# Sixth tile of theta and sixth mixing step of batch 0 on split operands

## The chip, the cores and the metric

The kernel runs on one core of a Trainium2 chip. The metric is the time of one execution on the device in microseconds; the number given is the median of several runs. 0.5% of it is about 2.2 us.

## The reference

Four batches of 768 tokens, 8 heads of 64: local attention (a window of 16 to each side) together with attention to block summaries (maximum of k and mean of v over 32 tokens), then a mixing layer. All inputs are fp32.

```python
scores_l = scale * q @ k.T, kept where |s - t| < 16
scores_s = scale * q @ k_sum.T + log(32)
a = softmax over both;  x = a @ concat(v, v_sum)       # 768 x 512 a batch
theta = x @ w_theta
zr, zi = x * cos(theta), x * sin(theta)
y = w_tok_r @ zr + w_tok_i @ zi                        # over the tokens
u = x + y
out = u + max(u @ w_ch, 0)
```

## The kernel before

**Tiles and stages.** Each batch is 6 tiles of 128 tokens, so there are tiles 0 to 23. A tile goes through scores (L523), softmax on VectorE (L559) and ScalarE (L563), a transpose (L572, copied out at L578), the product with v (L546), normalisation (L586 to L598), a transpose of x (L605, copied out by L309 or L311), theta (L639 or L644), the phase (L655 to L669: rounding to whole turns, then two sines), and z = x times cosine and sine (L674, in two halves of the channels). The mixing of batches 0 and 1 (`mix_step`) takes two halves of the channels, each of six steps, one for every 128 tokens; step s needs z of tile s and the two weight blocks `w_tok_r` and `w_tok_i` of these rows. A step is four operations on TensorE. Batches 2 and 3 are mixed in `mix_fast`, with sums of weights made beforehand (`weight_sums`) and streamed from HBM through `s_scratch` (L817). At the end comes the product with `w_ch` (L922).

**Plain and split operands.** A product can be made in two ways. Plain: fp32 operands, one matmul instruction of the program, which the trace shows as two records. Split: each operand is a rounded part (`hi_op`, a cast, L309 or L311) and the rest (`lo_op`, a subtraction, L318), and three matmuls stand in place of one. The weights come as 64-bit floats and are first made fp32 on chip (`to_f32`: L401, L405, L407, L409, L412). Two numbers in TUNE say where the split starts: tiles from RT on have theta split, steps from RM on have z and weights split. Both are 6, so batch 0's six tiles of theta and the six steps of its first mixing half are plain; its second half is split already. The weights of theta are split ahead of tile RT (`theta`); those of a plain step are split after that step (`split_wt`), in time for the second half.

**Where things lie.** Fp32 weights of two blocks share one of twelve slots `wt`; from there each pair is written to `f_scratch` (768 KB), to be read by `weight_sums`. The temporaries of `to_f32` and the loads of k and v for the next batch's summaries (L444, L465) share three buffers `f`. Theta's fp32 weights lie in the four buffers `xh`, `xl`, which afterwards hold the split x. TensorE's results lie in PSUM; GpSimd does not read them.

**Order.** Every operation has a number, in the order in which the program states it. ORDER lists all numbers in the order of issue, with a letter where the engine is chosen by hand (a, d, g; without one, ScalarE where it can, then VectorE). Each engine works through its operations in that order, waiting for whatever one needs; all transfers are issued by one queue (SP), in that order too. Where VectorE and GpSimd both use SBUF (`port`), a GpSimd operation listed right after a VectorE one waits for it.

Of the kernel before, what the change touches and what calls it, by code (L numbers as in the profile page):

```python
# [17 lines left out]
B, H, S, D = 4, 8, 768, 64  # L18
# [36 lines left out]
17g 8 0g 1g 31 23 27 25 9 24 18 29 10 28 2 26 39 3 19 32 30 20 4 44g 33 5 6g 190g 49g 46 45 48 7 50 86 194g 47 193 51 60 61 34  # L55
35 52 53 79 191 64 239g 192g 87 57 55 62 54 66 13 88 65 185 11 93 14 42 238 63 89 12 36 241g 40 90 59 58 240g 91 100 67 56 80
195 37 38g 235 68 15 92d 188 186 81 69 107 21 82 204 94 71 205 206 108 41g 43d 70 83 209 290 207 95g 187 72 109 84 237 210 196
208 199 76 295g 198 73 197 294g 200 189g 74 77 22 242 203 96 101 75d 102g 201 202 78d 236 251 252 351g 254 212 211 103 213 97
253 104 85 98 215 214 110 223 216 296g 258 224 99d 225 243 255 257 217 118 348g 226 105 227 218 119g 220d 293 256 245 219d 106
244 246 228 247 250 111 120 221 291 121 249 222d 248 123 124g 297 229 122 349g 298 345 259 230 260 262 292 299 261 270 130 125  # L60
301 350g 115 300 271 263 126 272 303 423g 305 302 304 306 273 267d 308 131g 307 116 264d 419 310 135 268 309 265 274 313 127
136g 132 311 312 266d 141 275 269d 314 276 133 315 142g 137 317 316 277 138 352 143 112 231 325 326 318 232 134 327 163 233g
139 144 353 361 168 319d 356 328 320 329 362 278 330 322 355 234 169g 145 331 346 164g 321d 279 364 323 363 282 117 146 324
283 420 332 354 113 347 284 280 365 474 285 147 380 358 114 357 339 165 360 148 366 359 337 166 367 338 149 167 170 368 150
152 381 424 369 422 333 370 400 153 382 128 383 384 171 334 154 172 155 157 281 158g 156 425 385 371 402 401 159 372 386 340
174 335 175g 373 426 392 394 374 421 160 375 377 376 378 387 529 161 404 176 388 379 403 705g 389 454 177 530 179 395 393 178
# [12 lines left out]
795 838g 756 1015 757 690 528g 571 845g 975 765 662 822 759 760 976d 850 691 840 977d 578 846 978 851g 796 768 823 727d 763
184 797 852 946 699 766 758 692 853g 769 1020 701 694d 979 940 702 980 700 941 847g 772 848 693d 579 981 825 767 695 749 696d  # L80
761 762 771 731 753 750 764 580g 798d 824 982 728 770 732 773 983 774 775d 984 947 956 581g 776 854g 777 995 948 729 778d 959
849 781d 949 950 958 725g 582g 802 952 803 996 997 998 953 799g 859 751 943 1016 1021 779 951 782 855 999 730 780 1074 1000
985 860g 1001 856 800 726 963 1018 808 857 1002 942 954 861g 957 961 960 962 801 955 575 826g 783 964 862 863g 1077 858 944g
965 1003 1022 966 1004 986 967d 864g 968 1005 806 804 1017g 810 1031 972 868 805 865g 1050 828 1023 1051d 1052 1032 869g 573
577 987 829 1170 1053 830 1024 866 1025 1033 989g 1006 969d 1054 827 1035 1037 831 1029 1055 870 1028 993 871 1056 1007g 970
872g 1027 1034 867 973 1120d 1038 1008 877 994 1036 1026 1057 1019d 1058 1013 1030 971 1014 974d 873d 1059 1039 874g 1040 1042
1078 878 1041d 809 811 990g 1079 1043 1047d 1208 1076 807 1087 1089 991 876 992 1209 1088 1090 1011 1210d 1083 1094 1093 1044d
1060 879 1009 880 1211 1080 1212 875 881 1082 1129 1012 1045 882g 1048 1213 886 1061 1126 1081 1092 1066 883 1075 1010 884
1084 1091 1214 1063g 1085 887 1067 885 1062 1127 1121 1046d 988 888 1215 1086 1173 1068 1049 1216 895 1095 1096 1098 1106g
1130 1217 1097d 889 1099 1218d 1279 1107g 1280 1281g 1069 1131 1070 896 1071 1228 1133 1100d 1282 1064g 1219 1135 890 1103d  # L90
1229 1283 1072 1073 1139 1065 891g 1137 1132 1110 1141 892 1142 1101 1284 1111 897 1143 1104 1285 1134 1138 1102d 898g 1108
1105d 1145 899g 1146 1286 1140 1144 1136 1109 1287 1128 893 900d 1158d 1147 1148 901g 1150 894 1288 1172 1250 1149d 1118 1174
1289 1114 1175 1112 1151 1305 1116 1178 1179 902 1202 1236 1122 1152 1183 903 1221g 1123 1306 1124 1185 1307 1308g 1187 1177
1181 1309 1153 904 1182 1160 1184 1232 1310 1155 1189 1237 1230 1233 1220g 1188 1176 1125 1186 1311 905 1156 1162 1171 1290
1312 906g 1249 1154 1163 1203 1247 1190 1180 1157 1234 1313 1159g 1191 1192 1193 1291g 1231 1251 1314 1222g 1194d 907 1315d
1252 1254 1195 1235 1292g 1117 1354 1240 1196 1253 1355 1260 1261 1356 1161 1199d 1255 1357g 1166 1168 1319 1197 1358 1198d
1322 1256 1257 1241 1258 1164d 1165g 1169 908g 1316 1263 1242 1200 913 1359 1206 1264 1360 1259 1207 1201d 1243 909 1324 1361
1167 1262 1248 1317g 1267 1382 1599g 1266 1268 1265 1362 1269 910g 1325 1326 1363 1271d 911 1364d 1270 1327 1272 16 1368 1600g
1335 1238 1204 1226 1330 1369d 914g 1328 1463 1370d 1365 915 1387 1276 1371 1366 1205 1367g 912 1273d 1331 1334 1372 1224 1338
916 1595g 1373 1225 1274 1337 1239 1383 1587g 1374 1223 1329 917 1385 1275 1244 918g 919 1245 1293 1596g 1277 1375 1376 1227  # L100
1278 1377 1588g 1333 1388 1320 920 1332 921 1589d 1246g 1339 1294 1297 1321d 1384 1378d 1417 931 1336 1295 1342 1296 1418 1341
1419g 1323 1420 1389 922 1672 1340 1593 1301 1594 1113 1119 1343 923g 1590 1318g 1344 1644 1346 932g 1421 924g 1345 1302 1646
# [71 lines left out]
class Program:  # L174
# [5 lines left out]
    WINDOW, WARM, COOL = 3.41, 0.88, 0.45  # L180
# [99 lines left out]
def attn_moe(tc, qg, kg, vg, kT, vT, vn, wth, wtr, wti, wch, out, tune=TUNE):  # L280
# [4 lines left out]
    K = tune  # L285
# [4 lines left out]
    f_dram = nc.dram_tensor("f_scratch", (NT, P, 2 * S), F32, kind="Internal").ap()  # L290
# [6 lines left out]
    pr = Program()  # L297
# [825 lines left out]
```

## Time and profile before

| | us |
|---|---|
| median of 3 runs | 435.23 (433.77 to 435.77) |
| the profiled execution | 437.3 |
| its span, first to last instruction | 435.6 |
| TensorE busy | 421.7 |
| VectorE busy | 352.2 |
| ScalarE busy | 280.3 |
| GpSimd busy | 209.7 |

The span is 1.7 us shorter than the profiled execution's time. Busy times of TensorE are of pipelined matmuls, with modelled ends, so a full engine is not one at its peak.

### The profile page before, as it was taken

To read this page: it belongs to the slowest core of one execution; us is meant where nothing else is said; L and a number is where in the kernel's file an instruction comes from. 1 tells how busy PE (TensorE), PEld (TensorE's weight loads), DVE (VectorE), ACT (ScalarE), POOL (GpSimd) and SP (SyncE) were. 2 spreads that over 40 slices of the span, in tenths; PEclk is the share of its full clock that TensorE was granted. 3 is DMA by queue.
4 is the path that set the end of the run, shared out by engine and by line. 5 is a ranking of instruction groups with operands and counts; after the bars stand their busy time and mean duration, and the time that the engine had idled before them with its cause. 6 is when DMAs were issued, how large, how long until landed. Compare 5 with 4: busy or idle time off the path is not lost.

```text
span 435.6 us, 10044 instructions
## 1 busy us (share of the span) xinstructions
PE 421.7 (97%) x3682; PEld 350.9 (81%) x3682; DVE 352.2 (81%) x947; ACT 280.3 (64%) x600; POOL 209.7 (48%) x208
## 2 busy tenths in 40 slices
PE   5989999998999999999999999999999989999996
PEld 1455555665888888888888899999899989999996
DVE  3799999778988777875757695866489989999996
ACT  1799995787757784866785885493955447455210
POOL 3543324687775665245465578624453410251542
PEclk9899999999999999999999999999999999999999
DMA  8999956989678678848767987883379696220138
GB/s 294 347 354 364 295 197 208 290 257 322 230 233 273 197 224 266 259 139 247 232 188 223 292 273 218 245 246 119 111 230 338 229 367 223 75 73 20 65 136 289
DMA packets 76321, 100.07 MB, mean 230 GB/s; under 512 B 23024, under 2 KB 58864, under 8 KB 76272
## 3 DMA queue, kind: packets, MB, share of 16 engines
q1 hardware_dynamic: 76272, 99.43, 71.1%
q8 instruction: 29, 0.48, 0.5%
q14 instruction: 20, 0.16, 0.1%
HBM read 75.82 MB, written 23.59 MB: 228 GB/s over the span
## 4 chain that ended last, share of the span: by engine, by line
PE 87%; DMA 10%; DVE 1%; ACT 1%; SPq 0%; issue 0%; POOL 0%; DVEq 0%
PE m L702 25%; PE m L817 19%; PE t L644 11%; PE c L922 7%; PE m L922 6%; PE pa L546 5%; PE s L523 4%; PE t L639 3%; PE t L605 3%; DMA q<-qg 3%; PE pa L572 3%; DMA wth<-wth 2%; DMA wt<-wti 2%; DMA zu<-kT 2%; DMA wt<-s_scratch 1%; PE t L922 1%
## 5 line engine op out<-in xcount | busy, mean ns | idle before, releaser
L817 PE MATMUL m<-wt,hl 128*128 128x384 f32 x504 | 95.7, 339 | 1.4 <-DMA wt<-s_scratch 1.2
L817 PEld LDWEIGHTS m<-wt,hl 128*128 128x128 f32 x504 | 87.7, 188 | 4.9 <-ACT hl L309 1.5
L702 PE MATMUL m<-wt,hl 128*128 128x512 f32 (+1 forms) x432 | 84.9, 341 | 0.0
L702 PEld LDWEIGHTS m<-wt,hl 128*128 128x128 f32 x432 | 68.6, 188 | 10.8
L563 ACT ACTIVATE e<-e,st 128x118 f32<-128x118 f32 x192 | 63.1, 388 | 12.1 <-DVE st L559 11.6
L559 DVE CUSTOM_DVE_ANT_0 e<-s,cs 128x118 f32<-128x118 f32 x192 | 46.8, 272 | 9.6 <-PE s L523 4.7
L318 POOL TENSOR_TENSOR hl<-zu,hl 128x512 fp32r<-128x512 f32 x23 | 30.1, 1309 | 43.9 <-DMA wt<-s_scratch 15.9
L644 PE MATMUL t<-wth,xh 128*128 128x512 f32 x144 | 45.3, 396 | 0.0
L674 POOL TENSOR_TENSOR zu<-xn,zu 128x512 f32<-128x512 f32 x20 | 27.0, 1350 | 20.3 <-ACT zu L668 5.5
L657 DVE SCALAR_TENSOR_TENSOR zu<-zu,t 128x512 f32<-128x512 f32 x24 | 16.4, 684 | 24.4 <-ACT zu L655 24.4
L702 PE MATMUL m<-wt,zu 128*128 128x512 f32 (+1 forms) x96 | 33.4, 491 | 1.2 <-DVE zu L674 1.2
L655 ACT ACTIVATE zu<-t,bmagic 128x512 f32<-128x512 f32 x24 | 16.5, 687 | 23.9 <-PE t L644 18.3
L309 ACT CAST hl<-zu 128x512 fp32r<-128x512 f32 x31 | 19.1, 619 | 18.2 <-PE m L817 14.9
L702 PEld LDWEIGHTS m<-wt,zu 128*128 128x128 f32 x96 | 17.5, 190 | 15.8 <-issue 12.6
L546 PEld LDWEIGHTS pa<-v,e 118*64 118x64 f32 x768 | 24.8, 137 | 6.8 <-issue 3.0
L318 DVE TENSOR_TENSOR hl<-zu,hl 128x512 fp32r<-128x512 f32 x37 | 27.6, 751 | 2.3 <-ACT hl L309 2.1
L523 PE MATMUL s<-k,q 64*64 64x118 f32 x768 | 25.6, 272 | 3.9 <-POOL cs L340 3.2
L546 PE MATMUL pa<-v,e 118*64 118x65 f32 x768 | 28.1, 224 | 1.2 <-ACT e L578 1.2
L730 POOL TENSOR_TENSOR zu<-zu 128x512 f32<-128x512 f32 x15 | 21.4, 1432 | 15.0 <-DVE zu L730 4.9
L644 PE MATMUL t<-wth,xl 128*128 128x512 f32 x72 | 28.6, 397 | 0.0
L674 DVE TENSOR_TENSOR zu<-xn,zu 128x512 f32<-128x512 f32 x28 | 24.7, 884 | 4.8 <-ACT zu L668 4.6
L523 PEld LDWEIGHTS s<-k,q 64*64 64x64 f32 x768 | 20.2, 135 | 9.2 <-POOL cs L343 4.0
(181 smaller groups left out, 909.9 us busy)
## 6 DMA issues: line engine op xcount, KB each, us to landing
wt<-s_scratch SPq DMA_DIRECT2D x48, 384.0 KB, 4.4
v<-vg SPq DMA_DIRECT2D x48, 195.0 KB, 5.3
s_scratch<-f SPq DMA_DIRECT2D x24, 384.0 KB, 3.9
k<-kg SPq DMA_DIRECT2D x18, 376.0 KB, 5.5
q<-qg SPq DMA_DIRECT2D x24, 256.0 KB, 6.0
wt<-wtr SPq DMA_DIRECT2D x6, 768.0 KB, 11.0
wt<-wti SPq DMA_DIRECT2D x6, 768.0 KB, 11.4
f<-kT SPq DMA_DIRECT2D x12, 384.0 KB, 4.3
```

The lines of the kernel that those rows point to most:

```text
L309: nc.scalar.copy(dst(), src())
L318: lambda e: V[e].tensor_tensor(dst(), src(), hi().bitcast(F32), op=ALU.subtract), reads, writes, due, port=BOTH)
L523: mm(0.79 * len(pairs) / NP, [lambda p=p, g=g, h=h: nc.tensor.matmul(sc[h].get()[ROW[g], p], q.get()[ROW[h], p, ROW[g]], k.get()[ROW[h], p ...
L546: mm(2 * 0.433 + scores[0] + (0.2 if scores[0] else 0.0), [lambda n=n, g=g, a=a: nc.tensor.matmul(xa[a].get()[ROW[g], n], turned[g].get()[ ...
L559: op({"DVE": 0.205}, lambda eng, n=n: nc.vector.tensor_tensor_reduce(e()[:, n], sc[n % 2].get()[:, 2 * a + n // 2], mask(m), -SCALE, 3.0e3 ...
L563: op({"ACT": 0.288}, lambda eng, n=n: nc.scalar.activation(e()[:, n], e()[:, n], AF.Exp, bias=st.get()[:, n:n + 1], scale=-1.0), [(st, n)] ...
L644: calls = [lambda t=t, xx=xx, k=k, c=c: nc.tensor.matmul(th.get(), xx.get()[:, c], w_th[c].get()[:, k], start=(c == 0 and t == 0), stop=(c ...
L674: op({"DVE": c_dve(DM, "two"), "POOL": c_pool(DM)}, lambda e, z=z, hc=hc: V[e].tensor_tensor(z(), xn[b, i].get().rearrange("p h d -> p (h ...
L702: nc.tensor.matmul(acc[th](), zz, w[:, TT[th]], start=(s == 0 and r == 0 and t == 0 and (th == 0 or c == 0)), stop=(s == NT - 1 and r == 1 ...
L730: lambda e: V[e].tensor_tensor(dst(), x(), y(), op=ALU.add if sign > 0 else ALU.subtract), reads, writes, due, port=BOTH)
L817: calls = [lambda ref=ref, tt=tt, z=z, s=s, j=j, t=t, x=x, k=k, bank=bank, first=first: nc.tensor.matmul(bank[j].get()[:, :HT], z.get()[:, ...
L922: calls = [lambda k=k, t=t, x=x, y=y: nc.tensor.matmul(to.get(), weights[n][x][0]()[:, k, j * P:(j + 1) * P], operands[n].get()[:, y, k], ...
```

## The change

RT and RM become 5. Tile 5's theta and step 5 of the first half of batch 0 then use split operands. Tile 5 of x gets a cast and a subtraction, and so does the first half of the channels of its z. The weights of theta are split ahead of tile 5. The two weight blocks of step 5 are made fp32 in a buffer `f`, split at once into two slots `wt` (before, after step 5), and written to `f_scratch` from there, one by one; what reads that row of `f_scratch` now waits for both. One copy, which keeps a weight of step 5 whose slot is needed, is now made for one of step 4. Operations: 2297 instead of 2292.

```diff
-... RT=6,RM=6, ...
+... RT=5,RM=5, ...
```
```diff
 def weight_sums():
...
                 dma(lambda f=f: f.get().rearrange("p (q c) -> p q c", q=4),
-                    lambda s=s, cols=cols: f_dram[s]..., S * 512, [("fd", s)],
+                    lambda s=s, cols=cols: f_dram[s]..., S * 512, [("fd", s)] + [("fd2", s)] * (s >= K["RM"]),
...
         else:
             f, f_ref = to_f32(NC + j, landed[j], S, 1e6)
+            if K["STR"] < B:
+                pr.key = ("FD", j)
+                dma(lambda j=j: f_dram[j // 2].rearrange("p (r c) -> p r c", r=2)[:, j % 2], f, S * 512, [f_ref],
+                    [("fd", j // 2) if j % 2 == 0 else ("fd2", j // 2)], 1e6, 3072, 0.55, 0.9)
             split_wt(j, (f, (f_ref, None)))
```

ORDER is another list from its first word on:

```diff
-17g 8 0g 1g 31 23 27 25 9 24 18 29 10 28 2 26 39 3 19 32 30 20 4 44g 33 5 6g 190g 49g 46 45 48 7 50 86 194g 47 193 51 60 61 34
...
+23 8 24 27 9 0g 1g 17g 18 25 29 2 28 26 10 44 3 46g 4 30 48g 19 45g 20 5 47g 86 14 21 6 49 39 50 15 7 31 195 87d 88g 33 51 52
...
```

With the numbers put back to operations, by the order in which the program states them:

| | before | after |
|---|---|---|
| operations on TensorE, VectorE, ScalarE, GpSimd, SP | 548, 755, 497, 204, 288 | 548, 773, 487, 200, 289 |
| first transfers | v, k x4, q, v, theta weight, v, theta weight | k x4, theta weight, q, v x2, theta weight, v |
| VectorE: operations ahead of its part of tile 3's phase (L657) | 127 | 134 |
| TensorE from tile 5's theta to step 5 | theta 5, product with v of 6 in between; transpose 7, step 4's last, x 6, product with v of 7, scores 8, three of theta 6, step 5 | theta 5, product with v of 6 in between; transpose 7, scores 8, x 6, product with v of 7, step 4's last, theta 6 (four), step 5 |
| split x and z of tile 5 | none | VectorE |
| splitting step 5's weights | after step 5 | first: GpSimd; second: ScalarE and GpSimd; both ahead of step 4 |

In that table theta's numbers are of tiles; one operation of theta is a quarter of the tile's product.

## Rows read from the trace of the kernel before

**Rows 1.** The page: busy time, share, instructions by engine; the chain that ended last, by engine.
```profile
PE 421.7 (97%) x3682; PEld 350.9 (81%) x3682; DVE 352.2 (81%) x947; ACT 280.3 (64%) x600; POOL 209.7 (48%) x208
...
PE 87%; DMA 10%; DVE 1%; ACT 1%; SPq 0%; issue 0%; POOL 0%; DVEq 0%
```
**Rows 2.** Busy time by stretch: length, five engines with instructions, clock, DMA share, GB/s.
```profile
45.00:50.00 5.00, 5.00 (x15) 2.58 (x14) 5.00 (x16) 4.98 (x13) 2.78 (x3) 1.00 1.01 322
...
80.00:85.00 5.00, 4.93 (x102) 3.48 (x104) 3.04 (x23) 2.72 (x9) 4.19 (x6) 1.00 0.98 321
```
**Rows 3.** TensorE's timeline: start, length, instructions, idle time before them and what ended it.
```profile
10.92 1.78 PE L523 MATMUL s<-k,q 64*64 64x118 f32 x32 [3.25 <-POOL cs L340]
...
39.44 1.04 PE L523 MATMUL s<-k,q 64*64 64x118 f32 x32 [0.44 <-DMA q<-qg]
...
81.06 1.04 PE L523 MATMUL s<-k,q 64*64 64x118 f32 x32
...
99.98 1.56 PE L702 MATMUL m<-wt,zu 128*128 128x512 f32 x4 [1.23 <-DVE zu L674]
...
351.48 2.32 PE L817 MATMUL m<-wt,hl 128*128 128x384 f32 x12 [1.20 <-DMA wt<-s_scratch]
```
**Rows 4.** The chain that ended last, in order of time: start, length, what.
```profile
68.77 3.43 PE t L639 x8
72.20 6.45 PE m L702 x20
...
120.69 3.19 PE m L702 x18
...
127.36 1.39 PE t L644 x6
```
**Rows 5.** Groups by line and shape: busy us, mean ns, idle before.
```profile
L318 DVE TENSOR_TENSOR hl<-zu,hl 128x512 fp32r<-128x512 f32 x37 | 27.6, 751 | 2.3 <-ACT hl L309 2.1
...
L318 DVE TENSOR_TENSOR xl<-x,xh 128x512 fp32r<-128x512 f32 x15 | 10.7, 713 | 5.2 <-POOL xh L311 3.2 <-ACT xh L309 1.9
...
L311 DVE CAST hl<-zu 128x512 fp32r<-128x512 f32 x13 | 6.7, 524 | 0.0
...
L318 POOL TENSOR_TENSOR wt<-wt 128x768 fp32r<-128x768 f32 x8 | 15.3, 1917 | 4.7 <-DVE wt L311 2.7 <-DVE wt L318 2.0
...
L311 POOL CAST wt<-wt 128x768 fp32r<-128x768 f32 x4 | 3.6, 908 | 0.1
```
**Rows 6.** Timeline of the sync queue, the first issues.
```profile
0.82 0.45 SPq L303 DMA_DIRECT2D x<-vn  x1
1.32 1.88 SPq L303 DMA_DIRECT2D zu<-kT  x4
```
**Rows 7.** VectorE's timeline, its first waits.
```profile
5.50 0.95 DVE L446 TENSOR_REDUCE ks<-zu 128x24 f32<-128x768 f32 x1 [4.51 <-DMA zu<-kT]
7.89 2.94 DVE L446 TENSOR_REDUCE ks<-zu 128x24 f32<-128x768 f32 x3 [1.43 <-DMA zu<-kT]
...
12.85 0.28 DVE L559 CUSTOM_DVE_ANT_0 e<-s,cs 128x118 f32<-128x118 f32 x1 [1.89 <-PE s L523]
```
**Rows 8.** ScalarE's timeline, phase of tile 5.
```profile
91.92 0.69 ACT L655 ACTIVATE zu<-t,bmagic 128x512 f32<-128x512 f32 x1 [0.67 <-PE t L639]
...
95.05 1.28 ACT L667 ACT_TABLE_LOAD   x1
```
**Rows 9.** VectorE's timeline, two products with x.
```profile
77.54 0.68 DVE L674 TENSOR_TENSOR zu<-xn,zu 128x512 f32<-128x512 f32 x1
...
97.62 2.30 DVE L674 TENSOR_TENSOR zu<-xn,zu 128x512 f32<-128x512 f32 x1
```
**Rows 10.** GpSimd's timeline.
```profile
79.32 0.40 POOL L500 COPY k<-ks 128x192 f32<-128x192 f32 x1 [2.39 <-DVE ks L446]
...
97.55 1.83 POOL L318 TENSOR_TENSOR wt<-wt 128x768 fp32r<-128x768 f32 x1
```
**Rows 11.** DMA issues by kind: times, KB each, median us from issue to landing.
```profile
s_scratch<-f SPq DMA_DIRECT2D x24, 384.0 KB, 3.9
```

More of the change, by code (lines that the diff above doesn't have):

```diff
@@ new lines @@
+503 555 549g 504 505d 526 558 556 747 506 750 562 596 550 507 239g 527 560 511 563 564 559 508 565 557 566 568 528 509 512
+510d 561 551g 404g 567 513d 140 569 529 570 530 751 571 572 600 573 531 716 574 532 575 667g 717d 718d 576d 719 582g 738 539
+533 720 609 721 597 601 637 579 602 722 723 603 534 536d 537 598 292 607 611 606 577 752 610 578 580 584 604 724 583g 753 585
+744 614 586 581d 608 629g 605 615 634 612 587 616 294g 739 588 617 678 837 681 590 613 618 619 635 620d 725 638 621 594 789
@@ new lines @@
+846 689 823 712 824 945 732g 841 714 545 546 825 699 842g 700 702d 844 843g 761 701 826 827 703 770 980 762 981d 946 766 982g
+847 758 759 715 845 950 707d 708 983 713 764 763 704d 1020 848 771 800 775 772 773 734 855 984 849 801g 735 774 765 985 705
+828 850g 1026 731 802 706d 776 736 733g 986 737 767 851d 987 754 803d 807 768 951 852 805 856 830g 857g 858g 769 808 709 988
+777 989 755 853 1000 1001 806 804 778 815 811 779 781 1002g 952 854 780d 1021 756g 809 864 782 859g 953 833 947 990 813 957
@@ new lines @@
+1003g 860d 991 865g 861 862 786d 863 961 1004 834 948 1079 954 956 965 955 958 866 867g 959 992g 868 964 869g 1005 835 1006
+836 963 993 783 960 968 1007 962 787 784 1023 785d 967 996 788d 969 949g 966 970 829 873 1008 870g 971d 972 1027 1009 1024d
+1028 871 831d 810 874 973 1055 1056 974 1036 1039 977d 1057 1031 1082 882 872 997 832 812 975 998 814 595 1016 1040 1058 1175
+1059 1032 875 1017 876g 1038 883 978 1060 1061 999 1029 1062 1033 994g 884 1043 1035 877 1030 1037 1080 878d 880 1018 1022
@@ new lines @@
+885g 879g 1034 816 1111g 976d 1041 1042 979d 1044 995 1045 1010 886 591 1063 881 1046 887g 1047d 1083 1064 1048 1049d 1092
+1094 1213 1084 1011 1019 1052d 1087 1086 1214 1093 1095 1178 888g 890 1012g 1215 1216 1065 891 1073 1014g 1071 1217 889 1090
+1096 1013g 1015g 892g 1074 1099 1218 1050 900 1072 893g 1219 1075 894g 1081 1131 1220 1053 1077 1134 1088 1051 1098 895 896d
+1078 1085 1054d 1066 1221 1089 1222 1067g 1091 897 1284 1285d 1076 1097 1069g 1286g 1100 898 1101 1223 1070 1068g 1103 1135
@@ new lines @@
+1287g 1102d 1136 1139 1104 1144 899 1125d 1113 1224 1137 1288 1140 1105d 1233 1114 901g 1132 1138 1146 902 1106 1289 1141 1108
+1109 903g 1145 1133 1241 1126g 1107d 1150 1143 1110d 1290 1234 1147 1115 904g 1291 1142 1149 1151 1148 1292 905d 1117 1242
+906g 1116 1169 1112g 1225g 1152 1153 1252 1155 1154d 1179 1119 1255 1293 1235 1188 1192 908 1156 1294 1176 1123 1118 1163d
+1190 1310 1121 909 1180 1127 1183 1160 1311 1236 1187 1312 907 1128 1181 1295 1157d 1313 1182 1161 1239 1191 1226g 1296g 1164
@@ new lines @@
+1594d 1122 1328 1608 1595g 1395 1428 1304 1351 1350 1652 1429 1308 1430 1352 1616g 1601g 1386 1302 1663 1431 936 1665 1397
+1356d 1307 1353d 1683 1432 1649 1654 1385g 1651 1403 1405 1354 1406 1433 1357 1653 1409 1303 1124 1355d 1401 1399 1667 926
+1396 1410 929g 937 1655 1434g 1400 1398 1404 1596g 1656 1389d 1440 1402 1358d 1408 930 1471 1597 1411 1407 1412 938g 1500 1435
+1657 1658 1441 1677 1413 1414 1309 1659 1415 1612 1602d 931 1438 1603 1609g 1443 1449 1532 1669 932 1419 1661 1416 1671 1664
@@ new lines @@
+1779 1632g 1731 1591 1635 1719 1780 1734 1521 1522 1550 1590g 1633g 1523 1524d 1525 1551 1552 1740 1636g 1785 1559 1562 1721
+1723 1732 1560 1716 1718 1554 1725 1727 1786 1720 1787d 1788g 1526d 1839 1564 1529d 1789 1729 1733 1548 1781 1790 1553 1638g
+1782 1743 1547 1736 1566 1527 1791 1555 1556 1735 1561 1792 1639 1722 1784 1783g 1565 1793 1530 1739 1746 1641d 1751 1528d
+1642 1794 1558 1557 1531d 1742 1738 1799 1563 1724 1800d 1567 1801d 1568 1802 1795 1643 1796 1741 1744 1745 1797 1569 1803
@@ new lines @@
+2066 1883 1993 2067 1994 2042 2078 1996 2061 2127 1997 2068 2000 2119 2123 2034 2177 2133 2124 2003 2074 2178g 1999 2136 2005
+2120g 2002 2075d 2186 2076 2004 2047 2046 2092 2079 2093 2048g 2081 2077d 2099 2097 2095 2070 2100 2082 2121 2083 2246 2096
+2128 2085 2102 2098 2089 2187 2125 2086 2103 2106 2179g 2140 2090 2122 2130 2104 2131g 2110 2087 2195 2137 2111 2157 2158
+2129g 2216 2180 2112 2138 2253 2107 2159 2139 2163 2132 2183 2161 2237 2164 2181 2088 2182 2105 2145 2142 2108 2188 2184 2134
@@ new lines @@
+2141 2162 2146 2149 2238 2160 2166 2170 2143 2153 2185 2147 2189g 2190g 2171 2167 2154 2221 2168 2155 2196 2239g 2197 2150
+2174 2276 2175 2200 2202 2198 2217d 2199d 2218 2191 2193 2243 2223 2151 2248 2240 2205 2148 2201 2241d 2084 2172 2192 2194
+2255 2219 2109 2209 2222 2230 2206 2224 2220 2242g 2144 2165 2210 2213 2244 2245g 2203 2231 2101 2152 2226 2214 2227 2281 2247
+2234 2228 2215 2257 2207 2256 2250g 2260 2211 2235 2258 2277 2169 2204 2278 2251 2283 2232 2249g 2229 2282d 2259 2261 2279
@@ L141 @@
+2262 2212 2280d 2208 2252 2263 2265 2254g 2284 2266 2286 2091 2287 2269 2173 2273 2288 2267 2080 2176 2270 2271 2285 2236 2264
+2289 2290 2268 2274 2291 2225 2272 2294 2233 2292 2275 2295 2293 2296
 """
@@ L740, in weight_sums @@
                 dma(lambda f=f: f.get().rearrange("p (q c) -> p q c", q=4),
[L741 removed]
+                    lambda s=s, cols=cols: f_dram[s].rearrange("p (q c) -> p q c", q=4)[:, :, cols], S * 512, [("fd", s)] + [("fd2", s)] * (s >= K["RM"]),
                     [(f, n) for n in range(4)], 1e6, HT * 2, 0.6, 0.55)
```

136 lines of the change are left out of this document (49 added, 87 removed).

## Prediction

> **What bounds the kernel.** I read the page's busy times and chain of waits first, then the busy times by stretch, then the timeline of each engine up to 110 us. TensorE is busy 97% of the span and holds 87% of the chain that ended last [rows 1], at its full granted clock: 1.00 (2.4 GHz) in every stretch shown [rows 2]. From 39.44 us on it stands almost still nowhere: its timeline has two holes of over a microsecond, 1.23 us before step 5 of batch 0's first mixing half (it waits for z) and 1.20 us at 351 us (it waits for a streamed weight) [rows 3]. So after 40 us an instruction less on TensorE is worth its own time, unless another engine can't follow. The engine that may not follow is VectorE: in the conversion of the weights it is as full as TensorE, 5.00 of 5.00 us from 45 to 50, with ScalarE at 4.98. After 80 us there is room: VectorE 3.04 of 5.00 us, and GpSimd, at 4.19, is the fuller one for a moment [rows 2].
>
> **What it removes from TensorE.** Theta of tile 5 is four fp32 products of 512 columns (two records each); eight such records took 3.43 us where nothing stood between them [rows 4]. Split, it is twelve records; six took 1.39 us, so twelve take 2.78. Gain 0.65 us. Step 5 of the first half is four fp32 operations of four records; twenty records took 6.45 us, so sixteen take 5.16. Split, they are four operations of six records; eighteen took 3.19 us, so twenty-four take 4.25. Gain 0.91 us. Together 1.56 us, 0.36%. These are durations of the same shapes beside the same neighbours at the same clock, so their bounds are narrow: the heads of such groups differ by about 0.1 us, twice.
>
> A rule gives more. Fp32 runs here as 3.43/4 = 0.86 us for 512 columns, the three split products as 0.70: a ratio of 0.81 [rows 4]. The Trainium skill, "FP8 and Floating Point Precision", section "TensorE Precision Notes", has true fp32 make four passes through the array, which makes three split passes cost three quarters. By it, 3.43 and 5.16 us would become 2.57 and 3.87, a gain of 2.15 us. The rows differ from it, so the sum goes by them.
>
> **What it adds elsewhere.** Tile 5 of x is split (cast 0.52 and subtraction 0.71 us, on VectorE) and so are the first halves of its z (cast 0.52, subtraction 0.75 us) [rows 5]: some 2.5 us of VectorE between 80 and 100 us. The cover is that stretch's idle time, 1.96 us in the first five microseconds alone [rows 2]; without it each would stand on TensorE's path at its own length. The two weights of step 5 are split some 30 us earlier than before, one by GpSimd's cast and subtraction (0.91 + 1.92 us) and one with ScalarE's cast; nothing but step 5 waits for them, and GpSimd has idle time there. I cost them at nothing on the path. Their write to the scratch tensor becomes two transfers of 384 KB in place of one of 768 KB, the same bytes. The split of theta's four weights comes one tile earlier; it was not what TensorE waited for.
>
> **What the new order moves.** It is new from its first word, so I compared the queues, not the words. On TensorE the operations from tile 3's scores to step 5 are nearly the same sequence; so the queues that feed it matter.
>
> At the start, the sync queue sends the four k transfers ahead of the first 512 KB of v, which came first [rows 6]. At the 322 GB/s of a full stretch [rows 2] that is 1.6 us. VectorE waited 4.51 and 1.43 us for k, and 1.89 us for the first scores [rows 7]; it should start up to 1.6 us sooner and have the conversion of theta's second weight to fill the last wait: a lead of 1.6 us, of 3.5 if that wait goes too. Against this it gets more to do in front: 134 instructions instead of 127 stand ahead of its part of tile 3's phase. At its mean (352.2 us over 755 operations, 0.47 us) that is 3.3 us; as the added ones are mostly conversions of 768 columns, it may be 4. A lead and a load of about one size: if the added ones only fill waits, 1.6 us are gained; if the lead stays 1.6 and the load 4, step 3 gets its z 2.4 us later. I take zero, as the middle of the load (3.6) is the longer lead (3.5).
>
> Ahead of step 5: tile 5's phase began on ScalarE at 91.92 us, had to load the sine table (1.28 us) [rows 8], and its z was there when TensorE went on at 99.98 us: 8.06 us, of which TensorE worked 8.06 - 1.23 = 6.83. After the change z must also be split, 0.52 + 0.75 = 1.27 us more; and TensorE has one more operation of tile 6's theta in front, 0.70 us more. The hole would be 8.06 + 1.27 - 7.53 = 1.80 us instead of 1.23, a loss of 0.57. Yet the product with x took 2.30 us on VectorE there, where the same form took 0.68 us at 77.54 [rows 9]; GpSimd began a subtraction of 1.83 us at 97.55 us, 0.07 us ahead of it [rows 10]. Without such a neighbour the hole closes (a gain of 1.05 to 1.23 us); with one for the subtraction too, another 1.6 us is lost. I take zero between these ends, since both kinds of neighbour stand in the rows.
>
> A rule bears on this place. The Trainium skill, "SBUF — State Buffer", section "Who interferes with whom", says that a VectorE instruction with two inputs in SBUF and a GpSimd instruction that reads SBUF shut each other out, the later one waiting fully. The 2.30 us agree: 0.68 after the 1.62 that the other had left is what would come out. It speaks against the change, whose added subtractions are of just that kind.
>
> **The sum.** The profiled execution took 437.3 us, of which 435.6 are its span; minus 1.56 gives 435.7. The median of the three runs shown is 435.23, 2.1 us below that execution, so the forecast for a median is 435.23 - 1.56 = **433.7 us**. A measurement tells some 0.5% (2.2 us) from no change, so the whole gain lies within that.
>
> **Rivals.**
> First, the stalls go as well. The order closes the hole ahead of step 5 (1.23 us), or the lead of VectorE at the start (1.6 us or more) reaches TensorE, or the stall at 351 us (1.20 us) goes. For it speak the k transfers in front; against it, the seven instructions. With one or two of the three: 430.8 to 432.5, say 431.7 us.
>
> Second, slower: the buffers. The float weights of step 5 now lie in the three buffers that the loads of batch 1's k and v use, and stay there through a cast, a subtraction and the write to HBM, which I price by the one of the same size to the other scratch tensor: 0.91 + 1.92 [rows 5] + 3.9 us [rows 11] = 6.7 us each, where before a conversion needed one for its own length only. The last k load waits for such a buffer, and then the sync queue behind it, with q, k and v of the next tiles. In the profile GpSimd waited for the sum over k and copied it at 79.32 us for 0.40 us [rows 10]; the scores that need it ran at 81.06 [rows 3]. So there is 1.3 us to spare. If the load is later than that, tile 6's scores come late on TensorE by the excess, at most 6.7 - 1.3 = 5.4 us, and the gain is gone from an excess of 1.6 on. With the middle of it, 3.5 us: 437.2 us. Against it: the transfers before 80 us can still be early, as the weights' last landing is put further forward in the sync queue.
>
> Third, the split z and the lock cost 0.6 to 2.2 us at step 5: 434.3 to 435.8, say 434.9 us.
>
> Fourth, by four passes against three, 435.23 - 2.15 = 433.1 us. That is a mechanism of TensorE alone, and the rows show its price for both forms already.
>
> **Chances.** The forecast (433.7, itself within 432.4 and 435.2) 0.42; stalls gone 0.22; buffers 0.25; z late 0.08; four passes 0.03. Under 433.05 us (faster by over 0.5%) lie the second case, three tenths of the first and half of the last: 0.36. Over 437.4 lie some 0.17 of the 0.25 of the buffers. The rest, 0.47, is within 0.5%. For 8 in 10 the range goes from 430.8 (1.56 with two stalls of the three gone) to 438.0 (1.56 less, and a load late by 5.6, of which 4.3 reach TensorE), leaving out the worst of the buffers and the best of the stalls.
>
> **What would show it.** Twelve records of theta at about 0.23 us a piece for tile 5, and steps of about 1.06 us for step 5; if these are there and the time isn't, the hole is elsewhere. TensorE's timeline must be free of holes between 40 and 100 us: one ahead of tile 6's scores shows the buffers, one ahead of step 5 the z. VectorE's first score instruction ahead of 12.85 us, and step 0 ahead of 45.65, show the lead. The prediction is wrong if TensorE starts its dense part over 2 us earlier or later, or if the stretch after 100 us, which I take as it was, has new stalls: its order is new too, and I have compared there only how far the operations of one tile stand apart, which is nearly as before.

## The result

| | before | after |
|---|---|---|
| median, us | 435.29 (433.77 to 435.77, 4 runs) | 440.22 (437.52 to 441.66, 4 runs) |
| the profiled execution, us | 437.3 | 439.17 |
| its span, us | 435.6 | 436.8 |

The ratio is 1.0111, 95% interval 1.0077 to 1.0146: slower by 3.4 to 6.4 us, and above the forecast range (430.8 to 438.0). The two profiles differ by only 1.9 us, so both kernels were profiled once more (below): before at 435.02, after at 440.09.

The page of after, the parts of [rows 1]:

```profile
PE 422.4 (97%) x3694; PEld 353.7 (81%) x3694; DVE 356.7 (82%) x965; ACT 288.7 (66%) x594; POOL 210.4 (48%) x204
...
PE 84%; DMA 8%; DVE 4%; ACT 1%; SPq 1%; issue 0%; POOL 0%; DVEq 0%; POOLq 0%; ACTq 0%
```

TensorE's timeline of after, against [rows 3]:

```profile
37.81 1.02 PE L639 MATMUL t<-xl,x 128*128 128x512 f32 x2
41.18 1.10 PE L523 MATMUL s<-k,q 64*64 64x118 f32 x32 [2.35 <-DMA q<-qg]
42.22 1.12 PE L605 MATMUL t<-cs,xn 128*128 128x128 f32 x4
43.27 1.11 PE L572 MATMUL pa<-cs,e 64*118 64x64 f32 x16
44.30 1.67 PE L639 MATMUL t<-xh,x 128*128 128x512 f32 x2
...
102.72 4.40 PE L702 MATMUL m<-wt,hl 128*128 128x512 f32 x24
...
353.72 2.52 PE L817 MATMUL m<-wt,hl 128*128 128x384 f32 x13 [1.21 <-DMA wt<-s_scratch]
```

Three things are to be seen. Step 5 is 24 split records in one piece, with no wait in front: the hole of 1.23 us is gone. The wait for a streamed weight is still there (1.21 us). And tile 4's scores, at 39.44 before, start at 41.18 after a wait of 2.35 us for q, and the operations behind them are long: two records of theta take 1.67 us. The clock says why. Busy time by stretch, after (PEclk stands third from the right):

```profile
40.00:42.00 2.00, 0.82 (x32) 0.84 (x32) 2.00 (x4) 1.29 (x3) 0.47 (x1) 1.00 1.05 278
42.00:44.00 2.00, 2.00 (x29) 1.45 (x20) 2.00 (x4) 0.61 (x2) 0.00 (x0) 0.51 1.02 410
44.00:46.00 2.00, 2.00 (x11) 1.12 (x8) 1.42 (x2) 1.99 (x3) 0.00 (x0) 0.64 1.01 409
46.00:48.00 2.00, 2.00 (x6) 0.76 (x5) 1.46 (x2) 2.00 (x4) 0.00 (x0) 1.00 1.04 413
```

TensorE stood still for most of 40 to 42, and from 42 on it ran at half clock (1.2 GHz) for a time; in these stretches the kernel before had 1.00. Against the usual distances of the same operations that costs 1.5 us.

The sync queue has q's place. First before, then after:

```profile
27.66 0.33 SPq L303 DMA_DIRECT2D q<-qg  x1
28.36 0.33 SPq L303 DMA_DIRECT2D v<-vg  x1
31.35 0.33 SPq L303 DMA_DIRECT2D wt<-wtr  x1
```
```profile
24.03 0.35 SPq L303 DMA_DIRECT2D wt<-wti  x1
24.75 1.02 SPq L303 DMA_DIRECT2D wt<-wtr  x2
28.23 0.33 SPq L303 DMA_DIRECT2D q<-qg  x1
```

Before, this q goes out ahead of a token weight of 768 KB (the `wtr` of 31.35 us); after, that weight (the second of the two at 24.75) is ahead of it. The DMA engines are full there (share 1.05), so what is put ahead should delay q by its own length: 768 KB at the 327 GB/s that they moved from 27 to 44 us take some 2.4 us, an estimate.

Where tile 3's scores, tile 4's, step 0, tile 6's scores and step 5 start on TensorE, in both profiles of each kernel:

| us | before | before again | after | after again |
|---|---|---|---|---|
| scores of tile 3 | 30.48 | 29.20 | 30.40 | 31.62 |
| scores of tile 4 | 39.44 | 37.89 | 41.18 | 42.42 |
| step 0 | 45.65 | 44.10 | 49.56 | 50.86 |
| scores of tile 6 | 81.06 | 79.37 | 84.95 | 86.24 |
| step 5 | 99.98 | 98.30 | 102.72 | 104.01 |
| end of the last matmul | 431.8 | 429.5 | 433.2 | 434.4 |
| span | 435.6 | 433.3 | 436.8 | 438.0 |

In the means, after is 1.2 us late at tile 3's scores, about as much as two profiles of one kernel differ there, and 5.3 us at step 0. From tile 3's scores to step 0, where the two profiles of a kernel agree within 0.3 us, it needs 19.2 us against 15.0. From step 0 to tile 6's scores both need the same 35.3 to 35.4 us. From there to the end after is 2.2 us faster (348.2 against 350.4). The span is 3.0 us longer, and the execution's time exceeds it by 2.1 to 2.4 us instead of 1.7.

### The profile page after: what moved, and what is told of

Read it like the earlier page. It is cut to its first block, busy times and chain, and to the rows that moved or that the text cites. A ratio compares the mean times of both kernels' runs of the same rounds, so it can differ in the third digit from the quotient of the medians.

```text
span 436.8 us, 10057 instructions
## 1 busy us (share of the span) xinstructions
PE 422.4 (97%) x3694; PEld 353.7 (81%) x3694; DVE 356.7 (82%) x965; ACT 288.7 (66%) x594; POOL 210.4 (48%) x204
## 4 chain that ended last, share of the span: by engine, by line
PE 84%; DMA 8%; DVE 4%; ACT 1%; SPq 1%; issue 0%; POOL 0%; DVEq 0%; POOLq 0%; ACTq 0%
PE m L702 25%; PE m L817 16%; PE t L644 11%; PE c L922 6%; PE pa L546 6%; PE m L922 5%; PE s L523 5%; PE pa L572 3%; PE t L639 3%; DMA q<-qg 3%; PE t L605 3%; DMA v<-vg 2%; DMA x<-vn 2%; DMA wt<-s_scratch 1%; PE t L922 1%; DVE hl L318 1%
## 5 line engine op out<-in xcount | busy, mean ns | idle before, releaser
L817 PEld LDWEIGHTS m<-wt,hl 128*128 128x128 f32 x504 | 87.7, 188 | 4.9 <-DMA wt<-s_scratch 2.0
L702 PE MATMUL m<-wt,hl 128*128 128x512 f32 x456 | 90.3, 341 | 0.0
L702 PEld LDWEIGHTS m<-wt,hl 128*128 128x128 f32 x456 | 72.3, 188 | 11.6
L674 POOL TENSOR_TENSOR zu<-xn,zu 128x512 f32<-128x512 f32 x26 | 35.3, 1360 | 42.8 <-ACT zu L668 17.6
L644 PE MATMUL t<-wth,xh 128*128 128x512 f32 x152 | 48.2, 399 | 0.0
L730 POOL TENSOR_TENSOR zu<-zu 128x512 f32<-128x512 f32 x12 | 16.3, 1358 | 28.0 <-DVE hl L318 15.7
L644 PEld LDWEIGHTS t<-wth,xh 128*128 128x128 f32 x152 | 25.3, 188 | 2.9
L702 PE MATMUL m<-wt,zu 128*128 128x512 f32 (+1 forms) x80 | 27.6, 492 | 0.0
L578 ACT COPY e<-pa 118x512 f32<-118x512 f32 x32 | 18.0, 584 | 13.5 <-PE pa L572 13.5
L318 POOL TENSOR_TENSOR wt<-cb,wt 128x768 fp32r<-128x768 f32 x6 | 12.2, 2038 | 28.7 <-DMA wt<-s_scratch 14.9
L309 ACT CAST hl<-zu 128x512 fp32r<-128x512 f32 x25 | 15.2, 617 | 15.5 <-PE m L817 12.6
```

Source lines behind the costliest of these rows:

```text
L318: lambda e: V[e].tensor_tensor(dst(), src(), hi().bitcast(F32), op=ALU.subtract), reads, writes, due, port=BOTH)
L578: lambda e, t=t, g=g: (nc.scalar.copy if e == "ACT" else nc.vector.tensor_copy)(t.get()[:NK], tp[g].get()[:NK].rearrange("k n q -> k (n q) ...
L644: calls = [lambda t=t, xx=xx, k=k, c=c: nc.tensor.matmul(th.get(), xx.get()[:, c], w_th[c].get()[:, k], start=(c == 0 and t == 0), stop=(c ...
L674: op({"DVE": c_dve(DM, "two"), "POOL": c_pool(DM)}, lambda e, z=z, hc=hc: V[e].tensor_tensor(z(), xn[b, i].get().rearrange("p h d -> p (h ...
L702: nc.tensor.matmul(acc[th](), zz, w[:, TT[th]], start=(s == 0 and r == 0 and t == 0 and (th == 0 or c == 0)), stop=(s == NT - 1 and r == 1 ...
L817: calls = [lambda ref=ref, tt=tt, z=z, s=s, j=j, t=t, x=x, k=k, bank=bank, first=first: nc.tensor.matmul(bank[j].get()[:, :HT], z.get()[:, ...
```

## The experiments

Each number that follows a label is a median of runs, with the ratio to runs of the kernel before on the same chip.

**The second profiles.**

> The kernel before, unchanged, for a second profiled execution. The first had a span of 435.6 us, where most of its executions have 432.7 to 434.6. Theory A: the operations start within 0.3 us of the first profile up to step 0, and the difference of some 2 us lies in one or two single waits elsewhere. Rival: the difference is in the start, and so the loss of the start is larger than the two profiles say.

> The changed kernel, unchanged, for a second profiled execution. Theory A: tile 4's scores wait for q again by over 2 us, half clock behind them, and step 0 starts at 49 to 50.5 us. Rival: the wait for q belongs to that one execution, and the loss lies in another place.

They gave 435.02 and 440.09 us (table above). Of the 2.3 us between before's two profiles, 1.55 lie in front of step 0 and 1.0 at the streamed weight of [rows 3] (that wait is 0.20 us now). So the rival there was mostly right, and the start's loss is larger than the first pair of profiles says: 3.9 us at step 0 in that pair, 5.3 in the means. In after's second profile the wait for q came back, 2.71 us, with clock 0.50 and 0.67 behind it: it belongs to the kernel.

**The old start, the new rest.**

```diff
-ORDER of after
+ORDER of before up to the first operation of step 0, then the rest in the order of after
```

> The changed kernel with the order of before up to the first operation of mixing step 0, and its own order from there. Theory A (the loss is made ahead of step 0: a late q of tile 4, the clock that falls in that wait, tile 3's transpose behind it; the split itself gains): step 0 begins at about 45.7 us as before, and the end comes 3.9 us sooner than in the changed kernel's profile, that is 1.56 us and a closed hole of 1.2 us better than before: some 432.7 us. Theory B (the split or the rest of the new order costs the time): the time stays at 439 to 440 us.

437.72 us, ratio 1.0056 (1.0040 to 1.0071). Step 0 came at 44.18, as early as before, but step 1 waited at the seam, and the clock fell behind that wait too:

```profile
51.74 4.54 PE L702 MATMUL m<-wt,zu 128*128 128x512 f32 x8 [2.13 <-DVE zu L674]
...
52.00:54.00 2.00, 2.00 (x4) 1.03 (x4) 1.60 (x4) 1.98 (x3) 0.37 (x1) 0.53 0.58 240
```

**The new order without the split.**

```diff
-RT=5, RM=5
+RT=6, RM=6    (after's order; the late splits of step 5's weights put back behind step 5)
```

> The new order with RT and RM at 6: tile 5's theta and step 5 plain again, their weights split after step 5 as before, everything else in the order of the changed kernel. Theory A: it loses what the split gains, 1.6 us, so it is slower than the changed kernel, about 441.8 us. Theory B with the split as the cost: faster than the changed kernel, 437 to 438 us.

448.1 us, ratio 1.0298 (1.0259 to 1.0337). It tells little: it waited 4.05 us for q of tile 4, but also 1.9 and 1.6 us for the late splits, which this order has no room for. That the new order costs more than the split gains fits it; the size doesn't follow.

**q ahead of the weight.**

```diff
-... 253 115 124g 260 ... 266 275 350 131g ...
+... 253 350 115 124g 260 ... 266 275 131g ...
```

> The changed kernel with one transfer moved: q of tile 4 is issued ahead of the weight of 768 KB that stood in front of it. Theory A: q lands some 2.3 us sooner, TensorE's wait of 2.35 us ahead of tile 4's scores goes nearly away and with it the half clock (about 1.5 us): 3 to 3.5 us sooner, about 436.9 us. Theory B: within 1 us of the changed kernel, because the weight that comes later is then what is waited for, or because the time goes elsewhere.

438.03 us, ratio 1.0063 (1.0041 to 1.0085): 2.2 us under after's median (by the two ratios 2.1 us, uncertain by 1.8). No wait for q, clock 1.00 from 40 to 46 us; tile 4's scores come 7.6 us behind tile 3's instead of 10.8. But then other things were late:

```profile
38.94 1.04 PE L523 MATMUL s<-k,q 64*64 64x118 f32 x32
41.31 0.66 PE L605 MATMUL t<-cs,xn 128*128 128x128 f32 x4 [1.34 <-DVE zu L657]
41.90 0.56 PE L572 MATMUL pa<-cs,e 64*118 64x64 f32 x12
43.33 0.33 PE L572 MATMUL pa<-cs,e 64*118 64x64 f32 x4 [0.86 <-ACT e L563]
```

Step 0 came at 48.51, 17.15 us behind tile 3's scores: 2.1 us more than before (15.0), and the waits of 1.34 and 0.86 us are about that.

**The wait filled.**

```diff
+    for _ in range(2):
+        mm(..., [lambda: nc.tensor.matmul(hold.get(), f_th[0][0]()[:, :P], f_th[0][0](), start=True, stop=True)], ...)
```

Two fp32 products of 512 columns that nobody reads stand ahead of tile 4's scores.

> The changed kernel with two more fp32 products of 512 columns on TensorE ahead of tile 4's scores (their result is not used), to keep it busy during the wait for q. Theory A: the wait stays, the clock does not fall after it, and step 0 begins about 1.5 us sooner: about 438.7 us. If the clock falls for another reason, or the two products are themselves in the way (1.7 us), the time stays at 440 or goes up.

438.19 us, ratio 1.0068 (1.0050 to 1.0086): 2.0 us under after's median (by the ratios 1.9 us, uncertain by 1.7), with two operations more on TensorE. The clock stayed at 1.00:

```profile
42.00:44.00 2.00, 1.93 (x21) 1.22 (x20) 2.00 (x4) 1.83 (x2) 0.00 (x0) 1.00 1.01 415
```

Step 0 started at 47.51, 2.05 us earlier, 0.69 of it by scores that started earlier; the rest is the clock.

**The old order up to step 2, the new one behind it; then q moved behind the weight there.** One operation (z of tile 2, 341) was put forward at the seam.

```diff
-ORDER of after
+ORDER of before up to the first operation of step 2, then the rest of after's        f1
```
```diff
-... 350 264 235 265 ... 355g 115 305 ...
+... 264 235 265 ... 355g 115 350 305 ...                                             f2, against f1
```

> The changed kernel with the old order up to the first operation of step 2 of the first mixing half, and the new order from there; one VectorE operation (z of step 2) stands at the seam where the old order has it, so that the seam has no stall of its own. Theory A (the split gains its 1.56 us and the whole loss is in the start): tile 4's scores at 39.4, step 0 at 45.7, step 2 at 62.9 us, no stretch at the half clock, no hole ahead of step 5, and a median of 435.46 - 1.56 = 433.9, or 432.5 with the hole of the kernel before (1.39 us) closed as well. Rival B (the split itself, or the new order behind step 2, costs time too): those starts, but 435.5 us or more.

> f1_late_seam with one thing changed: q of tile 4 is sent after the 768 KB weight that it stands ahead of in the old queue, as the new order has it. Theory A (that place in the sync queue made TensorE wait, and the wait made its clock fall): q lands about 2 us later, tile 4's scores start about 1.7 us later than in f1, half clock for some 3.4 us behind them, together 2 to 3.2 us more than f1. Rival B (the loss of the start is VectorE's load, and q was only what came last): under 0.7 us more than f1, and no stretch at the half clock.

f1: 438.29 us, ratio 1.0058 (1.0033 to 1.0084). f2: 441.03 us, ratio 1.0136 (1.0101 to 1.0172), 2.7 us more. Tile 4's scores in f1, then in f2:

```profile
40.12 1.04 PE L523 MATMUL s<-k,q 64*64 64x118 f32 x32 [0.94 <-DMA q<-qg]
```
```profile
41.27 1.39 PE L523 MATMUL s<-k,q 64*64 64x118 f32 x32 [2.87 <-DMA q<-qg]
```

In f2 they waited 2.87 us for q, with clock 0.50 and 0.69 in the two stretches behind; step 0 came 19.1 us behind tile 3's scores, in f1 15.9. (In f2 q also went behind one load of v, 195 KB, that stood between.) So theory A's mechanism is shown from both sides: the place in the queue costs 2 to 3 us. But f1 is not faster than before: it waited 1.83 us for tile 3's phase.

**The seam mended, twice.** f3 puts VectorE's and ScalarE's part of tile 3's phase ahead of conversions; f4 puts GpSimd's half of z of tile 3 ahead of the split of a weight, and six more operations forward.

```diff
+... 379 382 160 380 383 392 397 161 399 176 393 381 384 ...      f3: VectorE 160 380 383 392 161 176, ScalarE 379 382 393
+... 395g 180g 480 179 398 183 184 410 ... 185 186 440 ... 465 188 442 466 414 ...      f4: 395g, 183 184, 185 186, 465, 466 forward
```

> f1_late_seam once more, with the order at its seam set by hand: VectorE does the phase of tile 3 and ScalarE its part of it before the weight conversions and casts that stood ahead of them in f1, where TensorE waited 1.99 and 0.79 us. All else is as in f1: old order to step 2, the split, the new order behind. Theory A (the split gains its 1.56 us, the hole ahead of step 5 closes for another 1.39 us, and the loss was all in the start): f1's span of 436.2 us without the 2.8 us at the seam, 433.4, at a start as late as f1's (tile 3's scores at 30.4 us), and less for an earlier one; against the runs of the kernel before of the same call, -1.6 to -2.9 us. Rival B (the stalls move on, as they did in e1_old_start and f1: the order from step 2 on can't be fed from the old start): within 1 us of the kernel before or above it.

> f3_seam_mended with its two new waits taken out by order alone: GpSimd makes its half of z of tile 3 before it splits a weight of step 5 (0.82 + 1.84 us stood ahead of it), VectorE converts the last weight before a sum that waits for a load, and the phase of tile 4 stands ahead of a cast on ScalarE and two sums on VectorE. Old order to step 2, the split, the new order behind. Theory A (only places in the order cost time, the split gains): f3's span of 434.7 us without the 3.0 us of waits ahead of steps 3 and 4, 431.7, at a start as early as f3's; a median 1.0 to 2.5 us under the kernel before. Rival C (VectorE, ScalarE and GpSimd are so full up to 80 us that the splits made there cost their time wherever they stand: the wait has moved twice already, from step 1 to step 2 to step 3, and each time it was 3.0 to 3.4 us): a new wait of 2 to 3 us behind step 3, and a median 1.5 us or more above the kernel before.

f3: 437.79 us, ratio 1.0052 (1.0028 to 1.0075). f4: 439.16 us, ratio 1.0080 (1.0054 to 1.0106). Each mended its wait and got others. TensorE's waits between step 0 and tile 6's scores, f3, then f4:

```profile
73.40 5.43 PE L702 MATMUL m<-wt,zu 128*128 128x512 f32 x16 [1.81 <-POOL zu L674]
79.39 1.56 PE L702 MATMUL m<-wt,zu 128*128 128x512 f32 x4 [0.56 <-DVE zu L674]
```
```profile
77.68 1.56 PE L702 MATMUL m<-wt,zu 128*128 128x512 f32 x4 [1.65 <-DVE zu L674]
81.54 0.39 PE L470 MATMUL pa<-cs,vt 128*24 128x128 f32 x2 [2.08 <-DVE vt L466]
84.29 1.04 PE L523 MATMUL s<-k,q 64*64 64x118 f32 x32 [0.46 <-POOL k L500]
```

The wait of 2.08 us is for a sum over v. The transfers behind it, in the sync queue's timeline: before, then f4:

```profile
67.21 5.40 SPq L303 DMA_DIRECT2D f<-vT  x4
```
```profile
69.42 2.88 SPq L303 DMA_DIRECT2D f<-vT  x2
72.35 0.42 SPq L303 DMA_DIRECT2D v<-vg  x1
72.87 0.38 SPq L303 DMA_DIRECT2D f_scratch<-f  x1
74.65 1.68 SPq L303 DMA_DIRECT2D f<-vT  x2
```

Before, four loads of v go out within 5.4 us; in f4, where the float weights of step 5 lie in two of the three buffers `f`, the third and fourth wait until 74.65; the queue waited 2.1 us for GpSimd's subtraction, which reads such a buffer. That is the second rival of the prediction. In after the third and fourth load are no earlier (75.02), but TensorE comes to what needs them at 82.52 without a wait.

| scores of tile 6 | before (2) | after (2) | e1 | e3 | e4 | f1 | f3 | f4 |
|---|---|---|---|---|---|---|---|---|
| from tile 3's scores, us | 50.6, 50.2 | 54.6, 54.6 | 54.2 | 52.5 | 53.1 | 54.4 | 54.3 | 55.6 |
| from step 0, us | 35.4, 35.3 | 35.4, 35.4 | 39.5 | 35.4 | 35.4 | 38.5 | 38.5 | 40.0 |
| on to the end of the last matmul, us | 350.7, 350.1 | 348.2, 348.2 | 348.0 | 348.1 | 348.5 | 347.7 | 347.6 | 348.1 |

The last row shows what the change gains: in each kernel with both halves of the split and after's order there, the stretch behind tile 6's scores is 1.6 to 3.1 us shorter than in before's two profiles. All of the loss inside the span lies ahead of it. A part is made ahead of tile 3's scores: they come at 28.45 to 30.48 us in the eleven profiles with the old start (mean 29.5) and at 29.82 to 31.97 in the five with the new one (mean 31.0). No run here says by what.

With the old start (e1, f1, f3, f4) the earlier step 0 was given back before tile 6's scores each time, and the median came to 437.7 to 439.2 us where theory A had 432.5 to 433.9. So theory A, that the whole loss is in the start, fell: the late q and the clock behind it are real (e3, e4, f2), but behind an early start the changed kernel waits elsewhere.

**Theta's half of the change alone, on the old order.**

```diff
-RT=6, RM=6
+RT=5, RM=6
-ORDER: ... 448 493 449 451d 452 450d 453d ... 522 ... 536 509 ... 510 ... 708g
+ORDER: 708g ahead of 479g; 449 451d 452 450d 453d ahead of 490 492 491 484 493; 509, 510d and the two parts of x behind 522
```

> The kernel before with one half of the change: tile 5's theta on split operands, step 5 of the first half plain as before. The old order stays, except for what the split needs: theta's third weight is split by GpSimd some 10 us earlier, tile 5's x is turned, cast and subtracted on VectorE ahead of tile 7's scores, and for that the norm of tile 5 stands ahead of five maxima of tile 6. No weight of step 5 is split early and the buffers f are free as before. Theory A (a split saves TensorE its own time where its operands are there): twelve theta records in 2.78 us in place of 3.43, no new wait over 0.5 us, a median 0.65 us (0.2 to 1.1) under the kernel before. Rival C (VectorE, ScalarE and GpSimd are so full up to 80 us that any split brought forward costs its time there): a new wait of 1 us or more between 75 and 92 us, and a median 0.5 us or more above the kernel before.

436.91 us, ratio 1.0027 (1.0011 to 1.0042): a little slower, not faster. The twelve records are there, but TensorE waits in front of them and between them:

```profile
84.52 1.28 PE L523 MATMUL s<-k,q 64*64 64x118 f32 x32
85.73 0.98 PE L572 MATMUL pa<-cs,e 64*118 64x64 f32 x16
86.64 0.73 PE L644 MATMUL t<-wth,xh 128*128 128x512 f32 x2
87.21 0.40 PE L644 MATMUL t<-wth,xl 128*128 128x512 f32 x1
88.26 1.24 PE L546 MATMUL pa<-v,e 118*64 118x65 f32 x32 [0.66 <-issue]
```

From the third operation of step 4 to its fourth it needs 10.26 us, before 9.31. VectorE now has a copy, a cast and a subtraction of x between the maxima of tiles 6 and 7.

**What holds tile 6's scores.** h1 (on f4) and h3 (on the kernel before) let three of VectorE's instructions for each of the last two weights (limits, shift, first combination) work on 8 of 768 columns; h2 (on f4) fills the low parts of step 5's weights with zeros in place of a subtraction.

```diff
+        m = 8 if j in (14, 15) else n
-            f().bitcast(I32), f().bitcast(I32), 5, 2, ALU.logical_shift_left, ...
+            f().bitcast(I32)[:, :m], f().bitcast(I32)[:, :m], 5, 2, ALU.logical_shift_left, ...
```
```diff
+        if j in (14, 15):
+            op({"POOL": c_pool(n)}, lambda e: nc.gpsimd.memset(w.get()[:, 1].bitcast(F32), 0.0), [(w, 0)], [(w, 1)], due)
+            return w
```

> f4_seam_again, with part of the conversion of the last two weights left out: the limits, the shift and the first combination of W14 and W15 on VectorE work on 8 of 768 columns (their values are wrong). It takes about 3.5 us of work from VectorE between 62 and 71 us and changes no instruction, wait or place. Rival C, VectorE as the bound (98% busy there): TensorE's waits ahead of step 4 (1.81 and 2.26 us) fall by 2 us or more in sum, and the median by as much. The buffers: the wait of 2.26 us, for a sum over v whose load came late, stays; under 1.5 us of gain. Bad seams: under 0.7 us.

> f4_seam_again, with the subtraction that splits the weights of step 5 replaced by a fill with zeros on GpSimd (their low parts are left out): GpSimd reads neither the float weight nor its high part there, so it neither shuts VectorE out nor holds the buffers f that long. The buffers: the load of v comes 2 us earlier or more, the wait of 2.26 us goes, VectorE's combination of W15 takes 0.96 us and not 2.47, and the median falls by 2 us or more. VectorE as the bound: it gains the 1.5 us of the lock at most. Bad seams: under 0.7 us.

> The kernel before with the same part of VectorE's conversion of W14 and W15 left out as in h1. TensorE had no wait there, so nothing is expected: step 0 to step 4 stays at 31.54 us, the median within 0.5 us of the kernel before, unless the hole ahead of step 5 (1.2 us) closes.

h1: 437.70 us, ratio 1.0060 (1.0034 to 1.0086). h2: 438.07 us, 1.0068 (1.0043 to 1.0094). h3: 435.38 us, 1.0001 (0.9986 to 1.0016). The control is as expected: before, this work was hidden. The other two are below f4's 1.0080 by 0.9 and 0.5 us, but the intervals overlap (each difference is uncertain by some 1.6 us) and neither median brings the gain of 2 us or more. In the profiles TensorE's waits between step 0 and tile 6's scores fell from 4.19 us (f4) to 3.53 (h1) and 2.18 (h2), and that for the sum over v stayed (1.21 and 1.93). So neither VectorE's work alone nor the subtraction alone is shown to be what holds tile 6's scores, and that the four hand-made orders were merely bad ones is not excluded. One reason why h1 gained little is in its timeline of VectorE, with GpSimd's below:

```profile
62.99 0.15 DVE L408 TENSOR_SCALAR f<-f 128x8 int32<-128x8 int32 x1
...
66.44 0.67 DVE L406 TENSOR_SCALAR f<-f 128x8 f32<-128x8 f32 x1 [0.77 <-ACT f L402]
67.14 0.74 DVE L408 TENSOR_SCALAR f<-f 128x8 int32<-128x8 int32 x1
...
68.66 1.21 DVE L410 SCALAR_TENSOR_TENSOR f<-wt,f 128x8 int32<-128x8 int32 x1
```
```profile
65.82 1.27 POOL L675 TENSOR_TENSOR zu<-xn,zu 128x512 f32<-128x512 f32 x1 [3.68 <-DVE zu L675]
67.03 0.82 POOL L311 CAST wt<-f 128x768 fp32r<-128x768 f32 x1
68.03 1.81 POOL L318 TENSOR_TENSOR wt<-f,wt 128x768 fp32r<-128x768 f32 x1 [0.18 <-DMA v<-vg]
```

Eight columns take 0.15 us, but 0.67, 0.74 and 1.21 where GpSimd is at work, and each ends within 0.04 us of GpSimd's instruction: VectorE stood still for as long as the other had left. The Trainium skill, "SBUF — State Buffer", section "Who interferes with whom", has it so: the two share a pair of ports, and the later instruction is blocked fully. These rows agree.

## Why the prediction was wrong

**The sum was right, in its form and nearly in its size.** Theta of tile 5: the distances from operation to operation went from 1.05 + 2.77 us to 1.07 + 2.29, 0.46 us less (forecast 0.65). Step 5: before 1.21 + 2.58 + 1.38 = 5.17 us (forecast 5.16), after 4.33 (forecast 4.25), so 0.84 less (0.91). Together 1.30 us for 1.56. The price by the number of passes through the array (the fourth rival) did not come.

**The hole ahead of step 5** I set at zero between a gain and a loss. It closed: z's product took 0.69 us on VectorE, its cast 0.43 and its subtraction 0.69, with no GpSimd instruction beside them, and step 5 followed theta's last operation at once. VectorE, then GpSimd:

```profile
100.20 0.69 DVE L674 TENSOR_TENSOR zu<-xn,zu 128x512 f32<-128x512 f32 x1
100.93 0.43 DVE L311 CAST hl<-zu 128x512 fp32r<-128x512 f32 x1
101.39 0.69 DVE L318 TENSOR_TENSOR hl<-zu,hl 128x512 fp32r<-128x512 f32 x1
```
```profile
103.09 1.30 POOL L318 TENSOR_TENSOR hl<-zu,hl 128x512 fp32r<-128x512 f32 x1 [2.90 <-DVE wt L318]
```

That is 1.2 us on the good side. With the 1.30 of the split it makes 2.5 us, of which 2.2 are seen from tile 6's scores on. The third rival did not occur. (For the kernel before my text takes 1.62 us as what GpSimd's subtraction had left; its row has 1.83 - 0.07 = 1.76.)

**The step that failed is "a lead and a load of about one size … I take zero"**, the start. The lead did not reach TensorE: VectorE's first score instruction came at 11.55 us, against 12.85 [rows 7], but the second profile of before has it at 11.51, so it was no lead. The load was there, but TensorE did not wait for it where I had put it. Busy time by stretch from the start to VectorE's part of tile 3's phase and to tile 6's scores, before, then after (VectorE is the third number with a count behind it):

```profile
0.00:62.45 62.45, 55.17 (x522) 29.93 (x526) 52.26 (x167) 49.75 (x111) 23.41 (x46) 0.97 0.93 317
0.00:81.06 81.06, 73.72 (x607) 40.51 (x607) 68.54 (x203) 63.15 (x142) 32.32 (x55) 0.98 0.87 293
```
```profile
0.00:68.01 68.01, 58.76 (x538) 32.20 (x539) 57.00 (x174) 49.49 (x112) 23.49 (x46) 0.97 0.90 301
0.00:84.95 84.95, 75.70 (x607) 41.69 (x607) 70.74 (x207) 64.59 (x143) 34.92 (x57) 0.98 0.89 294
```

Ahead of its part of tile 3's phase VectorE has 4.7 us more to do (5.1 in the second profiles), where I put 3.3 to 4; up to tile 6's scores it has 2.2 us more (2.6), ScalarE 1.4 (1.6), GpSimd 2.6 (3.0). Yet behind step 0 TensorE waits for none of it in after. What stands last ahead of tile 4's scores is a transfer: I compared the first ten transfers and not q's place some 20 us later. In the means of both profiles it costs 2.2 us more wait than before, and the wait 1.5 us of clock: 3.7 of the 4.2 us by which after is slower from tile 3's scores to step 0. With one of the two repaired (e3, e4), 2.0 to 2.2 of the 4.9 us come back; in e3, where q is early, what is then late hangs on VectorE and ScalarE. "I take zero, as the middle" was a choice between two terms of 1.6 to 4 us each; the loss up to step 0 lay inside it, and a late start had no rival of its own with a chance. My text named the sign of it, "TensorE starts its dense part over 2 us … later", and it came: 3.9 and, in the second profiles, 6.8 us.

**"I cost them at nothing on the path"**, of the early splits of step 5's weights and theta's, is the other part. In after they cost nothing behind step 0 (35.4 us to tile 6's scores, as before). With the old start they did: step 0 came early and tile 6's scores did not. The buffers `f` (second rival) were held, and two loads of v came late for TensorE in f4; in after TensorE has no wait there. So a late start seems to cover what the early splits cost. Which part of that cost is buffers, which GpSimd's subtractions, which VectorE's work and which merely the places in a hand-made order, h1 and h2 leave open; a fourth buffer was not tried.

**The stretch after 100 us** has no new stall, as assumed. **Outside the span** after has 0.4 to 0.7 us more (439.17 - 436.8, 440.09 - 438.0, against 1.7). That does not go with the start alone: e1 and g1 have 1.7 and 1.8, f1 and f3, with the old start too, 2.4. Its cause is open.

None of the kernels tried beats the kernel before.

## What to carry over

Where a list of orders is made anew, compare every transfer that TensorE waits for by what stands ahead of it in its queue, up to the point where TensorE first runs without a wait; the first few say nothing of it. Work that is brought forward has to be made by somebody: while VectorE is 97% busy (30.74 of 31.55 us from step 0 to step 4 before), a split that saves TensorE 1.3 us can be paid for twice over by operations that come late (3.1 to 4.6 us up to tile 6's scores with the old start). And when a repaired start gives nothing, measure from a fixed operation to a fixed operation: here that showed the wait moving on each time.

## What was not expected of the hardware

A wait of TensorE cost more than its length: behind waits of 2.13, 2.35, 2.71 and 2.87 us (e1, after twice, f2) its granted clock was 0.50 to 0.53 in a stretch of two microseconds, and 0.61 to 0.69 in the one behind it. It did not always fall: behind the 2.08 us in f4 the stretches had 1.00, and in e4 two products that nobody reads, put into the wait, kept it there.
